# A decode attention kernel: x loaded once, first on the sync queue, its rows rebuilt on chip, and the last values load cut in two

## The chip, the cores and the metric

The kernel runs on one core of a Trainium2 chip. The metric is the device time of one execution in microseconds (us). Lower is better. The engines are named as in the profile: PE (matrix product), DVE (vector), ACT (scalar), POOL (GpSimd) and SP (the engine that only issues transfers here). ACT issues a few transfers as well.

## The reference

One token is decoded through an attention layer and a gating branch that read the same normalised input.

```python
x  = A_x                                   # (1, 1, 512), bf16
xn = layernorm(x)
# attention: 32 heads of 128, the last 4096 positions of the caches
q  = xn @ wq                               # 512 x 4096
s  = attention(q, k_cache[-4096:], v_cache[-4096:]) @ wo
# branch B: with one position the first half (gelu of xn@w1, shifted) is all zeros
x1 = xn + zeros @ w2
b  = x1 + gelu(layernorm(x1) @ w3) @ w4
out = x + s * silu(b)
```

The caches that are read are 32 heads x 4096 positions x 128 numbers, twice, in bf16: 67 MB of the 79 MB that the kernel loads. Everything is read once.

## The kernel before

**Tiling.** The 32 heads are worked in 8 groups of 4 (`G = 4`). For a group the keys come in one load of 4 MB: 128 partitions, each with 128 chunks (`CP = 128`) of 128 numbers, where 32 partitions belong to one head. The values come in the same shape. Part of a group's scores is made on DVE (`k_vector`, L321 multiplies keys by the broadcast query, L323 sums), part on PE (`k_turn`, L339 transposes, ACT copies at L342, `k_scores`, L350 multiplies). Then softmax, and `v_wide` (L427) multiplies values by the probabilities.

**Loop.** `for s in range(NG + LAG)` (L531) works on keys of group `s` and on values of group `s - 2` (`h`). Within the loop the order of PE, DVE and ACT is the written order (a manual schedule); ahead of the loop a scheduler orders the instructions. Each engine runs its own stream in order.

**Queues.** `load` (L75) issues a transfer on SP's queue and keeps the written order: w2, w3, w4, then keys of groups 0 to 2, values 0, keys 3, values 1 and so on. ACT's queue carries three transfers at the very start: `x_bf` (L79, x as 128 partitions x 4), `x_row` (L82, x as 4 rows of 128 on partitions 0, 32, 64, 96, into a tile that POOL has zeroed, L81) and `wq_sb` (L84, 4 MB). Completion is signalled through eight semaphore slots used in turn; a transfer that takes a slot again waits for the one before on it.

**Setup on the engines.** `x_bf` becomes `x_f` (L183), then the first layernorm gives `xn_bf` (L188). PE permutes it (L194, `xq_ps`), zeroes two banks (L145), and multiplies by wq (L208) to make the queries, which are copied, spread and broadcast into `q_bc` (L210 to L216). Branch B multiplies w2 (L233), takes a second layernorm (`z3_bf`, L239), multiplies w3 (L252), applies gelu, multiplies w4 (L270), and ends in `g_row` (L280). `x_row` is used twice: in `xn_row` (L242) and in the last addition (L653). The `wts` pool holds w2, w3, w4 and wq; the first values load reuses its space.

**The end.** The last group's values come in three loads, cut at `cuts = (0, 64, 96, CP)` (L526): 2 MB, 1 MB and 1 MB, followed by two loads of the last rows of wo (`wo_rows`, 256 KB each). The first two pieces go through `v_wide`, the last 32 chunks through `v_part` (L461), which multiplies one chunk per product:

```python
def v_part(g, v, c0, c1):
    s = st[g]
    for c in range(c0, c1):
        nc.tensor.matmul(s["oT"][:], lhsT=v[:, c, :], rhs=s["pT"][:, c, :], start=False,
                         stop=(c == CP - 1), skip_group_check=True)
```

Ahead of it on PE stand the transposes of the first pieces' sum (`v_turn`, L444) and eight products that add the other heads' output (L155 with `y_sum`). Behind it come `v_out` on DVE (L471), four heads' products with `wo_rows` (L155), the multiplication by `g_row` (L651), the addition of `x_row` (L653) and the store.

Of the kernel before, what the change touches and what calls it, by code (L numbers as in the profile page):

```python
# [8 lines left out]
P = 128  # L9
BF16 = mybir.dt.bfloat16  # L10
FP32 = mybir.dt.float32
ACT = mybir.ActivationFunctionType
ALU = mybir.AluOpType
AX = mybir.AxisListType
# [12 lines left out]
def kernel(  # L27
# [14 lines left out]
    nc = tc.nc  # L42
# [9 lines left out]
    CP = G * W // P  # L52
    PB = P // G
    KC = D // P
# [9 lines left out]
    small = ctx.enter_context(tc.tile_pool(name="small", bufs=1))  # L64
    ps_misc = ctx.enter_context(tc.tile_pool(name="ps_misc", bufs=1, space=PSUM))
# [7 lines left out]
    wts = wts_guard.__enter__()  # L73

    def load(dst, src):  # L75
        return tc.keep_in_program_order(nc.sync.dma_start(out=dst, in_=src))  # L76

    x_bf = small.tile([P, KC], BF16, name="x_bf")
    nc.scalar.dma_start(out=x_bf[:], in_=A_x.rearrange("a b (p c) -> p (a b c)", p=P))  # L79
    x_row = small.tile([P, P], BF16, name="x_row")  # L80
    nc.gpsimd.memset(x_row[:], 0.0)  # L81
    nc.scalar.dma_start(out=x_row[0:P:32, :], in_=A_x.rearrange("a b (j n) -> (a b j) n", j=KC))  # L82
    wq_sb = wts.tile([P, KC, HD], BF16, name="wq_sb")
    nc.scalar.dma_start(out=wq_sb[:].rearrange("p c n -> p (c n)"),  # L84
                        in_=A_wq.rearrange("(a b c) n -> b a (c n)", a=4, c=KC))
# [17 lines left out]
    ident_bf = const.tile([P, P], BF16, name="ident_bf")  # L103
# [12 lines left out]

    sel = wts.tile([P, PB, G], BF16, name="sel")
    nc.vector.tensor_copy(out=sel[:], in_=ident_bf[:, 0:P:32].unsqueeze(1).to_broadcast([P, PB, G]))
    ind = const.tile([P, 1], FP32, name="ind")
    nc.vector.tensor_reduce(out=ind[:], in_=ident_f[:, 0:P:32], axis=AX.X, op=ALU.max)  # L120
    neg_half = const.tile([P, 33], FP32, name="neg_half")
# [66 lines left out]
    nc.vector.tensor_copy(out=xn_bf[:], in_=xn_f[:])  # L188


    perm = wts.tile([P, P // 4, 4], BF16, name="perm")
    nc.vector.tensor_copy(out=perm[:], in_=ident_bf[:].rearrange("k (a b) -> k b a", a=4))
    xq_ps = ps_tr.tile([P, KC], FP32, tag="pt", name="xq_ps")
# [9 lines left out]
    for b in range(2):  # L203
        zeros(qr[b][:])
        for c in range(KC):
            wc = wq_sb[:, c, :].rearrange("p (g a d) -> p g a d", a=G, d=Dh)
            for a in range(G):
                nc.tensor.matmul(qr[b][32 * a:32 * a + 1], lhsT=xq_bf[:, c:c + 1], rhs=wc[:, 4 * b:4 * b + 4, a, :],  # L208
                                 start=False, stop=(c == KC - 1), skip_group_check=True)
    nc.scalar.copy(out=q_row[:, 0:4, 0, :], in_=qr[0][:])  # L210
    nc.vector.tensor_copy(out=q_row[:, 4:8, 0, :], in_=qr[1][:])  # L211
    for b in range(2):
        qb_ps = ps_tr.tile([P, 4, Dh], FP32, tag="pt", name="qb_ps")
        nc.tensor.matmul(qb_ps[:], lhsT=sel[:].rearrange("k b a -> k (b a)"), rhs=q_row[:, 4 * b:4 * b + 4, 0, :],
                         start=True, stop=True)
        nc.scalar.copy(out=q_bc[:, 4 * b:4 * b + 4, :], in_=qb_ps[:])  # L216
    for b in range(2):
# [5 lines left out]
        for t in range(2):  # L223
            rows = slice(64 * t, 64 * t + 64)
            nc.scalar.copy(out=q_pair[rows, 4 * b:4 * b + 4, :, G * t:G * t + G].rearrange("p g l a -> p g a l"),
                           in_=qt_ps[rows].bitcast(BF16).rearrange("p g (a m l) -> p g a m l", a=G, l=2)[:, :, :, 0, :])
# [4 lines left out]
    for j in range(KC):  # L231
        for c in range(KC):
            nc.tensor.matmul(hs_ps[:, j:j + 1], lhsT=w2_sb[:, c, j::4],  # L233
                             rhs=shifted_bf[:, c:c + 1], start=(c == 0), stop=(c == KC - 1))
# [30 lines left out]
    for i in range(11):  # L265
        n = P if i < 10 else 96
        terms.append((a_bf[0:n, i % 3, i // 3:i // 3 + 1], w4_sb[0:n, i, :]))
    for i, (col, w) in enumerate(terms):
        r = 32 * (i % 4)
        nc.tensor.matmul(hr_ps[r:r + 1].rearrange("r j n -> r (j n)"), lhsT=col, rhs=w, start=False,  # L270
                         stop=(i >= len(terms) - 4), skip_group_check=True)
# [25 lines left out]
                            op=ALU.max)  # L297
    par_t = const.tile([1 + G, PB, G], FP32, name="par_t")
    nc.vector.tensor_scalar(out=par_t[:],
                            in0=ident_f[0:1 + G, 1:1 + G].unsqueeze(1).to_broadcast([1 + G, PB, G]),  # L300
# [222 lines left out]
        rows_add(y_ps, o_blk[3][:, h - h_part:h - h_part + 1], wo_row(h), h == H - 1)  # L523

    NG = H // G
    cuts = (0, 64, 96, CP)  # L526
    region = tc.manual_schedule(engines={mybir.EngineType.PE, mybir.EngineType.DVE,
                                         mybir.EngineType.Activation})
    region.__enter__()
# [155 lines left out]
```

## Time and profile before

| | us |
|---|---|
| runs, median of 3 | 193.44 (193.44 to 193.47) |
| profiled execution, span from the first to the last instruction | 191.2 |
| what lies outside the span (median less span) | 2.2 |
| DVE busy | 150.9 (79% of the span) |
| PE busy | 116.4 (61%) |
| ACT busy | 89.2 (47%) |
| POOL busy | 2.3 (1%) |
| bytes moved by DMA | 79.02 MB, mean 413 GB/s |
| mean granted clock of PE | 0.72 |

The profile gives a span for the profiled execution and no separate device time for it, so the median stands for that. DMA's load does not appear among the engines' busy times: a line of the page gives the mean busy share of its 16 engines in 40 slices of the span, another what they moved in GB/s. In the timeline and the chain of waits, the first number of a line is its start in us from the span's start and the second what it took.

### The profile page before, as it was taken

Reading aid. Unit: us, or ns where it says so; the run is one execution under the profiler, and the core shown is the slowest. Engines: PE = TensorE matmul, PEld = TensorE weight load, DVE = VectorE, ACT = ScalarE, POOL = GpSimd, SP = SyncE. Lnnn points to the kernel's source line nnn. Section 1 sums busy time; section 2 is a strip of 40 time slices with the busy share of each in tenths; the row PEclk is TensorE's granted clock in tenths of the full one; section 3 lists DMA queues with packets and bytes.
Section 4 is the critical chain, followed back from the end, with each engine's and each line's share of the span. In section 5 each row is a group of like instructions: output and inputs, shape, how many; then the busy total and the mean of one; then the engine's idle time right before and its main releaser. Section 6 shows DMA issues by size and latency. Waiting matters only on the chain.

```text
span 191.2 us, 2839 instructions
## 1 busy us (share of the span) xinstructions
PE 116.4 (61%) x1159; PEld 74.2 (39%) x1159; DVE 150.9 (79%) x175; ACT 89.2 (47%) x191; POOL 2.3 (1%) x11
## 2 busy tenths in 40 slices
PE   1653754989825368256845772680888189739762
PEld 0430222767614334143334441540763077313322
DVE  1660159979999999999999999999999999980111
ACT  2001370888794076427464564542475148733120
POOL 2110000000000000000000000000000000000000
PEclk9999695555755557955695588557567858975998
DMA  6999999999999999999999999999999998999990
GB/s 211 447 430 404 431 418 439 439 439 437 432 434 439 432 429 432 432 439 432 422 432 432 418 422 418 452 439 435 439 432 434 435 432 372 471 425 405 420 371 32
DMA packets 4572, 79.02 MB, mean 413 GB/s; under 512 B 624, under 2 KB 1232, under 8 KB 1488
## 3 DMA queue, kind: packets, MB, share of 16 engines
q1 hardware_dynamic: 4264, 74.65, 91.6%
q10 hardware_dynamic: 296, 4.20, 5.1%
q8 instruction: 9, 0.15, 0.3%
q14 instruction: 3, 0.02, 0.0%
HBM read 78.84 MB, written 0.00 MB: 412 GB/s over the span
## 4 chain that ended last, share of the span: by engine, by line
DVE 46%; DMA 43%; PE 5%; ACT 3%; issue 1%; SPq 1%; ACTq 0%; DVEq 0%
DMA kv<-in_A_k_cache_dram 31%; DVE S L323 28%; DVE prod L321 15%; DMA kv<-in_A_v_cache_dram 10%; ACT kt L342 3%; DMA x_bf<-in_A_x_dram 2%; PE pt L339 2%; PE ov L427 1%; DVE m L366 1%; DVE S L364 1%; SPq L76 1%; PE sT L350 1%; DVE mx L374 1%; PE oT L461 1%; PE ot_ps L444 0%
## 5 line engine op out<-in xcount | busy, mean ns | idle before, releaser
L323 DVE TENSOR_REDUCE S<-prod 128x20 f32<-128x2560 bf16 (+1 forms) x32 | 86.0, 2686 | 1.1
L342 ACT COPY kt<-pt 128x1024 bf16<-128x1024 bf16 x52 | 51.2, 1013 | 40.4 <-PE pt L339 38.7
L339 PE MATMUL pt<-ident_f,kv 128*128 128x128 f32 x208 | 46.7, 376 | 10.8 <-DMA kv<-in_A_k_cache_dram 10.8
L321 DVE TENSOR_TENSOR prod<-kv,q_bc 128x2560 bf16<-128x2560 bf16 (+1 forms) x32 | 45.4, 1418 | 3.9 <-DMA kv<-in_A_k_cache_dram 3.7
L339 PEld LDWEIGHTS pt<-ident_f,kv 128*128 128x128 f32 x208 | 34.2, 196 | 14.4 <-DMA kv<-in_A_k_cache_dram 10.5
L350 PE MATMUL sT<-q_pair,kt 128*128 128x8 bf16 x416 | 19.4, 170 | 15.7 <-ACT kt L342 15.5
L350 PEld LDWEIGHTS <-kt 128*128 128x128 bf16 x416 | 16.4, 104 | 26.8 <-ACT kt L342 25.8
L427 PE MATMUL ov<-kv,pT 128*16 128x512 bf16 x248 | 22.0, 515 | 1.4 <-DMA kv<-in_A_v_cache_dram 1.4
L388 ACT ACTIVATE pT<-S,mb 128x128 bf16<-128x128 f32 x32 | 13.9, 573 | 0.3
L372 PE MATMUL mt_ps<-ident_f,m 128*1 128x128 f32 x8 | 2.9, 359 | 17.4 <-DVE rden L399 16.9
L433 ACT COPY ov_sb<-ov 128x512 f32<-128x512 f32 x8 | 4.7, 586 | 17.1 <-PE ov L427 17.1
L427 PEld LDWEIGHTS <-pT 128*16 128x16 bf16 x248 | 6.9, 109 | 13.2 <-issue 11.4
L359 ACT ACTIVATE own<-sT,par 128x48 f32<-128x48 f32 (+1 forms) x32 | 7.5, 356 | 3.7 <-PE sT L350 3.7
L444 PE MATMUL ot_ps<-ident_f,ov_sb 128*128 128x128 f32 x32 | 7.1, 359 | 2.9 <-ACT mb L384 1.9
L211 DVE CAST q_row<-qr_ps 128x512 bf16<-128x512 f32 x1 | 0.7, 692 | 9.9 <-PE qr_ps L208 9.9
L388 ACT ACTIVATION_READ_ACCUMULATOR pT<-S,mb 128x1 f32 x32 | 8.3, 258 | 0.0
L372 PEld LDWEIGHTS mt_ps<-ident_f,m 128*1 128x1 f32 x8 | 0.6, 80 | 17.9 <-DVE rden L399 17.2
L399 DVE RECIPROCAL rden<-den_ps 128x4 f32<-128x4 f32 x8 | 1.4, 175 | 7.0 <-PE den_ps L394 7.0
L381 PE MATMUL mb_ps<-md,par_t 5*128 5x4 f32 x16 | 3.9, 311 | 4.1 <-DVE md L376 4.1
L255 ACT ACTIVATE a_row<-a_ps 128x384 bf16<-128x384 f32 x1 | 0.5, 491 | 12.0 <-remote 12.0
L444 PEld LDWEIGHTS ot_ps<-ident_f,ov_sb 128*128 128x128 f32 x32 | 4.5, 178 | 3.9 <-ACT mb L384 2.3
L208 PE MATMUL qr_ps<-wq_sb,xq_bf 128*1 128x512 bf16 x32 | 3.1, 566 | 3.7 <-DMA wq_sb<-in_A_wq_dram 3.7
(122 smaller groups left out, 81.6 us busy)
## 6 DMA issues: line engine op xcount, KB each, us to landing
kv<-in_A_k_cache_dram SPq DMA_DIRECT2D x7, 4096.0 KB, 31.3
kv<-in_A_v_cache_dram SPq DMA_DIRECT2D x7, 4096.0 KB, 30.6
wq_sb<-in_A_wq_dram ACTq DMA_DIRECT2D x1, 4096.0 KB, 17.6
kv<-in_A_k_cache_dram SPq DMA_DIRECT2D x2, 2048.0 KB, 27.4
wo<-in_A_wo_dram SPq DMA_DIRECT2D x1, 2048.0 KB
kv<-in_A_v_cache_dram SPq DMA_DIRECT2D x1, 2048.0 KB
kv<-in_A_v_cache_dram SPq DMA_DIRECT2D x2, 1024.0 KB, 17.6
w_sb<-in_B_w_dram SPq DMA_DIRECT2D x1, 1376.0 KB, 9.1
```

What stands on the lines that cost most here:

```text
L321: nc.vector.tensor_tensor(out=prod[:, 0:m, :], in0=kn[:, rows, :], in1=q_bc[:, g:g + 1, :].to_broadcast([P, m, Dh]), op=ALU.mult)
L323: nc.vector.tensor_reduce(out=st[g]["S"][:, rows], in_=prod[:, 0:m, :], axis=AX.X, op=ALU.add)
L339: nc.tensor.transpose(pt[:, i, :], kn[:, c:c + 2, :].rearrange("p c d -> p (c d)").bitcast(FP32), ident_f[:])
L342: nc.scalar.copy(out=kts[b][:, 0:n, :], in_=pt[:, 0:n, :].bitcast(BF16))
L350: nc.tensor.matmul(st[g]["sT"][:, c:c + 2, :].rearrange("p c a -> p (c a)"), lhsT=kt[:, i, l::2], rhs=q_pair[:, g, l, :], start=(l == 0), ...
L359: nc.scalar.mul(s["own"][:, 0:m, a], s["sT"][:, 0:m, a], par[:, a:a + 1])
L372: nc.tensor.transpose(mt_ps[:], s["m1"][:], ident_f[:])
L381: nc.tensor.matmul(mb_ps[:], lhsT=par_t[:].rearrange("k b a -> k (b a)"), rhs=md[:], start=True, stop=True)
L388: nc.scalar.activation(out=s["pT"][:, :, a], in_=s["S"][:], func=ACT.Exp, scale=scale, bias=mb[:, a:a + 1], accum_out=s["sum"][:, a:a + 1])
L427: nc.tensor.matmul(ov[r:r + 4 * G], lhsT=s["pT"][:, c:c + 4, :].rearrange("p i a -> p (i a)"), rhs=v[:, c:c + 4, :], start=(i < 4), stop=( ...
L433: nc.scalar.copy(out=s["ov_sb"][:], in_=ov[:])
L444: nc.tensor.transpose(ot_ps[:, step * j:step * j + P], s["ov_sb"][:, j, :], ident_f[:])
```

## The change

`x_bf` is loaded by the first transfer on SP's queue. The transfer of `x_row` and the zeroing ahead of it are gone: DVE builds two masks from the identity, spreads `x_bf` by one of them, and one product on PE with the other gives x's four rows, each repeated on 32 partitions; DVE copies them into `x_row`. On ACT, wq is the first and only transfer. The last load of values is cut at chunk 112 into two loads of 512 KB, and `v_part` waits for the second only at chunk 112.

```diff
     x_bf = small.tile([P, KC], BF16, name="x_bf")
-    nc.scalar.dma_start(out=x_bf[:], in_=A_x.rearrange("a b (p c) -> p (a b c)", p=P))
-    x_row = small.tile([P, P], BF16, name="x_row")
-    nc.gpsimd.memset(x_row[:], 0.0)
-    nc.scalar.dma_start(out=x_row[0:P:32, :], in_=A_x.rearrange("a b (j n) -> (a b j) n", j=KC))
+    load(x_bf[:], A_x.rearrange("a b (p c) -> p (a b c)", p=P))
...
+    slot = wts.tile([P, PB], BF16, name="slot")
+    nc.vector.tensor_reduce(out=slot[:], in_=ident_bf[:].rearrange("k (a b) -> k b a", a=4), axis=AX.X, op=ALU.max)
+    part = wts.tile([P, 4], BF16, name="part")
+    nc.vector.tensor_reduce(out=part[:], in_=ident_bf[:].rearrange("k (a b) -> k a b", a=4), axis=AX.X, op=ALU.max)
+    same = wts.tile([P, 4, PB], BF16, name="same")
+    nc.vector.tensor_copy(out=same[:], in_=part[:].unsqueeze(2).to_broadcast([P, 4, PB]))
...
+    x_spread = wts.tile([P, PB, KC], BF16, name="x_spread")
+    nc.vector.tensor_tensor(out=x_spread[:], in0=x_bf[:].unsqueeze(1).to_broadcast([P, PB, KC]),
+                            in1=slot[:].unsqueeze(2).to_broadcast([P, PB, KC]), op=ALU.mult)
+    xr_ps = ps_misc.tile([P, P], FP32, tag="misc", name="xr_ps")
+    nc.tensor.matmul(xr_ps[:], lhsT=same[:].rearrange("k a b -> k (a b)"),
+                     rhs=x_spread[:].rearrange("k b c -> k (b c)"), start=True, stop=True)
+    x_row = small.tile([P, P], BF16, name="x_row")
+    nc.vector.tensor_copy(out=x_row[:], in_=xr_ps[:])
...
-    cuts = (0, 64, 96, CP)
+    cuts = (0, 64, 96, 112, CP)
```

The scheduler also moves instructions ahead of the loop. On PE, `rows_open` of `y_ps` (L149), the new product, the permutation (L194) and the two zeroing products (L145) now stand ahead of the 16 products with w2 (L233), where they stood behind them. On DVE the new instructions stand among the masks and around the copies of the first layernorm's result. From L208 on the streams of PE, DVE and ACT are as before, but for the added wait in `v_part`.

## The prediction

> **What bounds the kernel now.** I read the utilisation by slices first, then the same by windows, then the timeline at both ends and the chain of waits. The slices say that the DMA engines are full from the second slice to the last but one, near 430 GB/s:
>
> ```profile
> DMA  6999999999999999999999999999999998999990
> GB/s 211 447 430 404 431 418 439 439 439 437 432 434 439 432 429 432 432 439 432 422 432 432 418 422 418 452 439 435 439 432 434 435 432 372 471 425 405 420 371 32
> ```
>
> DVE is as busy in slices 10 to 34, and the chain of waits runs along DVE from 41.9 to 130 us. That is no contradiction: the two run side by side at nearly one pace, and both must be watched. The end goes by DMA. The chain's last pieces:
>
> ```profile
> 167.79 18.54 DMA kv<-in_A_v_cache_dram
> 186.33 0.05 issue
> 186.38 0.97 PE oT L461 x32
> 187.35 0.02 issue
> 187.37 0.17 DVE o L471
> 187.55 0.04 issue
> 187.59 0.42 PE y_ps L155 x16
> ```
>
> So the time is: when the stream of bytes starts, plus 79 MB at a fixed rate, plus the tail behind the last values (186.33 to 191.2). In the middle nothing is edited. The change can act only on the start, on the tail, and on DVE's start if that slips too far. The start by windows (busy sums per engine, granted clock, DMA share, GB/s):
>
> ```profile
> 0.00:2.00 2.00, 0.61 (x1) 0.10 (x1) 0.52 (x6) 0.00 (x0) 1.23 (x9) 1.00 0.24 29
> 2.00:4.00 2.00, 0.00 (x0) 0.00 (x0) 0.00 (x0) 1.04 (x1) 0.00 (x0) 1.00 0.93 306
> 4.00:6.00 2.00, 0.59 (x2) 0.50 (x2) 0.53 (x4) 0.24 (x1) 0.00 (x0) 1.00 1.01 419
> ```
>
> Between 2 and 4 us the engines are 93% busy but move 306 GB/s. By the packet records, w2's 4 KB packets take 0.159 us each once running, but the first on each engine takes 0.34 to 0.85. This start-up loss is about 0.6 us per engine. The timeline gives the issues and the consumers:
>
> ```profile
> 0.73 1.81 SPq L76 DMA_DIRECT2D w_sb<-in_B_w_dram  x4
> 0.74 0.40 ACTq L79 DMA_DIRECT2D x_bf<-in_A_x_dram  x1
> ...
> 1.18 1.11 ACTq L82 DMA_DIRECT2D x_row<-in_A_x_dram  x1
> ...
> 2.32 0.61 ACTq L84 DMA_DIRECT2D wq_sb<-in_A_wq_dram  x1
> ...
> 4.71 0.17 DVE L183 CAST x_f<-x_bf 128x4 f32<-128x4 bf16 x1 [3.38 <-DMA x_bf<-in_A_x_dram]
> ...
> 19.91 3.15 PE L208 MATMUL qr_ps<-wq_sb,xq_bf 128*1 128x512 bf16 x32 [3.74 <-DMA wq_sb<-in_A_wq_dram]
> ...
> 26.09 1.23 DVE L321 TENSOR_TENSOR prod<-kv,q_bc 128x2048 bf16<-128x2048 bf16 x1 [2.19 <-DMA kv<-in_A_k_cache_dram]
> ...
> 41.91 1.49 DVE L321 TENSOR_TENSOR prod<-kv,q_bc 128x2560 bf16<-128x2560 bf16 x1 [0.99 <-DMA kv<-in_A_k_cache_dram]
> ```
>
> DVE waits 2.19 us for the first keys and 0.99 us for the second load, then no more until 154 us.
>
> **Part 1: x and wq change queues.** ACT loses two DMA issues, so wq is issued near 0.74 instead of 2.32. On SP, x_bf takes the place at 0.73 and pushes w2, w3, w4 and the keys back by one issue, 0.4 us. What counts is when every engine has bulk packets. Before: packet records show w2's first packets at 1.74 to 2.06 (mean 1.87, 0.6 us behind the issue's end), plus 0.62 us of start-up loss: 2.49. The windows give the same: 29, 306 and 419 GB/s over 2 us each are 1.51 MB by 6.00, which at 430 take 3.51 us. After: nothing shows how soon ACT's wq would deliver. The near bound is w2's lag (first packet at 1.75, mean 1.9); the far one is x_bf's row on ACT, whose first packet came at 2.35, 1.2 us behind its issue's end. w2, now second on SP, caps that near 2.3. With wq's 32 KB packets the loss falls on the first packet alone, 0.4 by w2's first ones. So 2.3 to 2.7 against 2.49: between -0.2 and +0.2 us. I take -0.05, the middle.
>
> **Part 2: who shares the engines early.** Before, wq's packets start at 6.6, behind x_row; w2 and most of w3 have passed. Packet records show the two queues taking turns one packet at a time (8 bytes of x_bf, 4096 of w2, 8, 4096; later 32 KB of wq, 10 KB of w4). wq's 32 KB packets take 1.22 us. [...] After: eight wq packets per engine alternate with eight of w2, so w2 lands near 2.5 + 7 or 8 x (1.22 + 0.16) + 0.4 = 12.6 to 14 instead of 4.5; wq lands near 14 instead of 19.9. The first keys stay at 26, since the bytes ahead of them are the same.
>
> This is the dangerous part, as PE runs in order: the w2 products (L233), the second layernorm and the w3 products (L252) stand ahead of L208. From the rows: L233 starts with w2, +0.85 to x1, +4.5 to z3 (8.47 to 12.97; less now, as the zeroing products have moved ahead), +0.3 and 2.9 for L252, then L208 to q_bc 5.1 (19.91 to 25.02). Sum 13.4, so DVE could begin at 26.0 to 27.5 instead of 26.09. Of up to 1.4 us, 0.99 is taken by the wait before 41.91. At most 0.5 us reaches the last group, where PE waits 1.02 us for the last value load's first piece (181.50) after its warm-up products. Cost: nothing. Without that cover it is one for one.
>
> New waits: the second key load now waits for wq's completion, with the third key load and all values behind it on SP; 14 us is early, as SP's queue then holds bytes until past 30. x_f waits for x_bf as before.
>
> **Part 3: x_row on chip.** Two reductions (0.28 to 0.37, rows of L131 and L136), two copies (0.19 and 0.3), one product on DVE (0.35) and one on PE (0.27): some 1.5 us of DVE. It has no work from 14 to 20 us (the windows show 0.00), so this is hidden; without that cover it delays q_bc. The memset of x_row leaves an idle POOL.
>
> **Part 4: the halves.** The last 1 MB becomes two loads of 512 KB; the first lands some 1.2 us before 186.33. But PE is not free then. Its rows:
>
> ```profile
> 185.22 0.66 PE L444 MATMUL ot_ps<-ident_f,ov_sb 128*128 128x128 f32 x4 [0.69 <-ACT ov_sb L433]
> ...
> 185.81 0.40 PE L155 MATMUL y_ps<-y_sum,ind 128*1 128x128 f32 x8
> ...
> 186.38 0.96 PE L461 MATMUL oT<-pT,kv 128*128 128x4 bf16 x32 [0.17 <-DMA kv<-in_A_v_cache_dram]
> ```
>
> PE gets to L461 at 186.21, so of the 0.48 us that sixteen products take only 0.17 can be saved. Then the next is late: the second wo_rows load, issued at 169.1 and 18.5 in landing, arrives at 187.6, and y_ps needs it for its last two heads, from 187.59 + 0.20. Packets halve from 8 KB to 4 KB: 0.309 against 2 x 0.159 us, eight times per engine, so everything behind lands 0.08 later. Heads 30 and 31 then start at 187.73 instead of 187.79. Gain 0.06; bounds 0 and 0.17. [...]
>
> **Sum.** -0.05 - 0.06 = -0.11: a span of 191.1 instead of 191.2. The medians lie 2.2 us above the span (193.44), so 193.3, from -0.2 - 0.17 to +0.2: 193.05 to 193.65.
>
> **Rivals.** *x waits behind wq (slower).* If wq's packets are there as early as x_bf's, the turns put up to seven 1.22 us packets between x_bf's eight per engine: x lands near 2 + 8.5 + 0.5 = 11 instead of 4.7. PE meets L194 and the zeroing before L233, 5.7 us behind x, so from x at 8.3 on it decides. At 11 to 12.5, L233 starts at 17 to 18, DVE at 30 to 31.5; less 0.99 and less PE's 1.02 to 1.5 the end moves by 1.5 to 3: 195.5. For it: both issues start within 0.01 us. Against: x_bf came 0.6 us behind w2 at equal issue, time enough for 8-byte packets of 0.009 us. [...]
>
> *A late stream or a longer chain (slower).* wq comes as late as 2.35, its packets also lose time, w2 does not fill in; or Part 2's chain is 1.5 us longer than summed. Either costs 0.4 to 1: 194.0.
>
> *The start-up loss goes (faster).* wq delivers at 1.75 while x still slips through, with long packets losing 0.25: 2.1 instead of 2.49, -0.4, with the tail 192.9.
>
> *The halves do nothing*, wo_rows gating all: within the forecast.
>
> **Numbers.** Forecast 0.45, late x 0.17, late stream or chain 0.16, no start-up loss 0.22. About 0.2% (0.39 us) is what a measurement here can tell from no change: 193.05 to 193.83. Faster takes the early stream and the forecast's lower edge, 0.25; slower takes late x and most of the late stream, 0.30; same 0.45. The range 192.8 to 195.0 leaves out most of the late-x case and little below.
>
> **What would show it.** Right: x_f starts near 3 us, wq lands near 14, L233 starts at 12.6 to 14, DVE's first prod by 27.5, last values within 0.25 us of 186.33, L461 split by a wait, y_ps ending near 187.95. Wrong: x_f after 8 us; the first prod after 28; L427's wait at 181.5 gone; or 0 to 4 us moving clearly more or fewer than 0.67 MB.

## The result and the profile after

The change makes the kernel a little slower. Its median is 193.88 us (193.39 to 195.21, 22 runs) against 193.48 (193.13 to 193.95, 22 runs of before on the same chip); the ratio is 1.0031, 95% interval 1.0019 to 1.0042. Seven of the 22 runs took 194.3 us or more, and none of before's did. These seven are called the late runs below.

The profiled execution of after took 194.16 us, its span 192.0. The slices of the span, the mean busy share of the 16 DMA engines and what they moved, show a stream as full as before:

```profile
DMA  6999999999999999999999999999999999999980
GB/s 232 396 415 428 441 423 435 430 437 433 437 439 437 437 420 437 423 437 437 427 430 437 423 433 410 457 437 427 437 423 416 433 437 396 466 433 403 411 342 8
```

The start by windows (busy time of PE, its weight loads, DVE, ACT, POOL; granted clock, DMA share, GB/s) and by the timeline:

```profile
0.00:2.00 2.00, 0.61 (x1) 0.10 (x1) 0.52 (x6) 0.62 (x1) 1.09 (x8) 1.00 0.03 0
2.00:4.00 2.00, 0.59 (x2) 0.50 (x2) 0.72 (x5) 0.66 (x1) 0.00 (x0) 1.00 0.87 275
4.00:6.00 2.00, 0.72 (x3) 0.53 (x3) 1.28 (x9) 0.00 (x0) 0.55 (x1) 1.00 1.32 561
```

```profile
0.73 0.62 ACTq L81 DMA_DIRECT2D wq_sb<-in_A_wq_dram  x1
...
0.73 0.39 SPq L76 DMA_DIRECT2D x_bf<-in_A_x_dram  x1
...
2.50 0.17 DVE L186 CAST x_f<-x_bf 128x4 f32<-128x4 bf16 x1 [1.16 <-DMA x_bf<-in_A_x_dram]
...
14.74 0.69 PE L244 MATMUL hs_ps<-shifted_bf,w_sb 128*128 128x1 bf16 x16 [6.95 <-DMA w_sb<-in_B_w_dram]
...
26.23 1.23 DVE L332 TENSOR_TENSOR prod<-kv,q_bc 128x2048 bf16<-128x2048 bf16 x1 [1.12 <-ACT q_bc L227]
...
42.19 1.49 DVE L332 TENSOR_TENSOR prod<-kv,q_bc 128x2560 bf16<-128x2560 bf16 x1 [1.13 <-DMA kv<-in_A_k_cache_dram]
```

x is there 2.2 us earlier than before. w2's 4 KB packets take turns with wq's 32 KB packets, 1.21 us each, and w2 lands at 14.69. The queries are ready 0.1 us behind the first keys (26.13), and DVE still has a wait of 1.13 us ahead of the second load. So the start is nearly what it was. The end is not. The chain of waits no longer ends on the values:

```profile
187.23 0.95 PE oT L472 x32
...
188.20 0.17 DVE o L482
...
188.42 0.42 PE y_ps L158 x16
```

The last values landed at 186.44, 0.11 us later than before, but PE came to them at 187.23. Before, it had waited for them. PE's rows of two earlier steps, the values of group 5 (L427 before, L438 after) and the first piece of the last values, show the lateness on its way, before first and then after:

```profile
164.60 1.90 PE L427 MATMUL ov<-kv,pT 128*16 128x512 bf16 x32
...
181.50 1.04 PE L427 MATMUL ov<-kv,pT 128*16 128x512 bf16 x16 [1.02 <-DMA kv<-in_A_v_cache_dram]
```

```profile
166.49 3.26 PE L438 MATMUL ov<-kv,pT 128*16 128x512 bf16 x32
...
183.04 1.04 PE L438 MATMUL ov<-kv,pT 128*16 128x512 bf16 x16
```

Before, the second row waited 1.02 us for data. In after it waits for none. The granted clock, the share of its full clock that PE was allowed (1.00 full, 0.50 half), was 0.50 from 152.2 to 169.3; before it had risen to 1.00 at 159.0. The windows of before (the third number from the end is the granted clock):

```profile
153.00:160.00 7.00, 6.19 (x50) 5.27 (x50) 6.86 (x9) 3.79 (x4) 0.00 (x0) 0.57 0.97 421
160.00:166.00 6.00, 4.80 (x83) 3.17 (x85) 5.53 (x7) 5.02 (x9) 0.00 (x0) 1.00 1.00 422
```

### The profile page after: what moved, and what is told of

The parts are those of the page before. It is cut to its first block, busy times and chain, and to the rows that moved or that the text cites. A ratio compares the mean times of both kernels' runs of the same rounds, so it can differ in the third digit from the quotient of the medians.

```text
span 192.0 us, 2845 instructions
## 1 busy us (share of the span) xinstructions
PE 118.7 (62%) x1160; PEld 75.4 (39%) x1160; DVE 152.2 (79%) x180; ACT 89.0 (46%) x191; POOL 2.2 (1%) x10
## 4 chain that ended last, share of the span: by engine, by line
DVE 47%; DMA 34%; PE 14%; ACT 3%; issue 1%; ACTq 0%; SPq 0%; DVEq 0%
DVE S L334 28%; DMA kv<-in_A_k_cache_dram 26%; DVE prod L332 15%; DMA wq_sb<-in_A_wq_dram 7%; PE ov L438 3%; PE pt L350 3%; PE yr_ps L529 2%; ACT kt L353 2%; PE ot_ps L455 2%; PE wm L518 1%; PE sT L361 1%; DVE S L375 1%; DVE m L377 1%; DVE mx L385 1%; ACT ov_sb L444 1%
## 5 line engine op out<-in xcount | busy, mean ns | idle before, releaser
L350 PE MATMUL pt<-ident_f,kv 128*128 128x128 f32 x208 | 47.5, 381 | 10.4 <-DMA kv<-in_A_k_cache_dram 10.4
L350 PEld LDWEIGHTS pt<-ident_f,kv 128*128 128x128 f32 x208 | 34.7, 198 | 13.9 <-DMA kv<-in_A_k_cache_dram 10.0
L438 PE MATMUL ov<-kv,pT 128*16 128x512 bf16 x248 | 24.3, 559 | 0.0
L438 PEld LDWEIGHTS <-pT 128*16 128x16 bf16 x248 | 7.2, 116 | 13.6 <-issue 12.7
L392 PEld LDWEIGHTS mb_ps<-md,par_t 5*128 5x128 f32 x16 | 3.3, 259 | 5.7 <-PE sT L361 4.2
```

The lines of the kernel that those rows point to most:

```text
L350: nc.tensor.transpose(pt[:, i, :], kn[:, c:c + 2, :].rearrange("p c d -> p (c d)").bitcast(FP32), ident_f[:])
L392: nc.tensor.matmul(mb_ps[:], lhsT=par_t[:].rearrange("k b a -> k (b a)"), rhs=md[:], start=True, stop=True)
L438: nc.tensor.matmul(ov[r:r + 4 * G], lhsT=s["pT"][:, c:c + 4, :].rearrange("p i a -> p (i a)"), rhs=v[:, c:c + 4, :], start=(i < 4), stop=( ...
```

## The experiments

All were compared with before on one chip in each group. Theory C says that PE's granted clock in the last keys' stage decides; the rivals stand in the expectations.

**Each half of the change alone.** `e1_halves` is before with after's cuts, `e2_x_only` is after with before's cuts.

```diff
-    cuts = (0, 64, 96, CP)
+    cuts = (0, 64, 96, 112, CP)
```

> The kernel before with only the last values load cut in two. Theory C (the granted clock of PE while the last keys are worked decides, and the early part of the change moves it): as before, 193.4, within 0.1 to 0.15 either way; last values at 186.4, L461 not before 186.2, so at most 0.17 won. Rival H (the halves themselves cost, by one more transfer and one more wait): 193.8, the whole loss.

> The changed kernel with the old cuts: only x, its rows and the queues are changed. Theory C: 193.8 to 193.9 with a wide spread, as the whole change; the products with the values of group 5 (L427 of before) start near 166 instead of 164.6 in runs that are late. Rival S (only the stream's later start counts): last values 0.1 later than before and 193.55. Rival H: 193.4.

Measured: the halves 193.79, ratio 1.0020 (1.0009 to 1.0032); x alone 193.80, ratio 1.0026 (1.0008 to 1.0044). For x alone that is what theory C said, and three of its twelve runs are late ones (up to 194.94). For the halves it is not: theory C said 193.4, within 0.15, and the median is the 193.8 of rival H. None of their runs is a late one, but three of twelve stand at 194.19 to 194.26, above all 35 runs of before in this group (up to 193.98). The end of the profile with the halves:

```profile
186.04 0.95 PE L461 MATMUL oT<-pT,kv 128*128 128x4 bf16 x32
187.25 0.72 PE L155 MATMUL y_ps<-wo_rows,o 128*1 128x128 bf16 x16 [0.26 <-DVE o L471]
```

The product of the last chunks starts 0.34 us earlier than before (186.38), and the sixteen products behind it then take 0.72 instead of 0.39, because the second load of `wo_rows` lands at 187.54. They end at 187.97, as before (187.98). So the halves gain nothing in this execution, which took 193.49. Why the median of this kernel is 0.2% up is not in its profile and stays open; f1 below, which has the halves too, shows no such cost.

**The early part in another order.** `e3_row_on_chip` is after with `x_bf` first on ACT, wq second there, and the old cuts. `e6_wq_on_sp` is after with wq on SP between w3 and w4.

```diff
-    load(x_bf[:], A_x.rearrange("a b (p c) -> p (a b c)", p=P))
+    nc.scalar.dma_start(out=x_bf[:], in_=A_x.rearrange("a b (p c) -> p (a b c)", p=P))
```

> x_row is made on chip, but x_bf stays the first load of ACT's queue, wq behind it, old cuts. x_bf takes turns with w2 as before, so w2 lands near 4.5 and L233's products run near 7. Theory C: the early PE work is back at its old place, so 193.4 to 193.5 with before's spread. If the making of the rows on DVE and PE costs: 193.8. If the missing x_row lets wq start near 4 instead of 6.6, nothing of it is seen at the end, since the engines were full.

> The kernel after with wq as a load of the SP queue between w3 and w4 instead of the first load of the ACT queue, so that x, w2, w3, wq, w4 and the keys follow each other in one queue and nothing shares the engines with w2. w2 lands near 5 us instead of 14.7, wq near 15 to 19, the second layernorm is as early as in before. With x_bf at 0.73 and w2 at 1.14 the first 4 KB packets come at 2.3, 0.4 us later than in before, and no other transfer fills that time: stream 0.3 later than in before, last values near 186.6. Theory C with the late w2 as what moves the clock: the runs above 194.3 are gone, median 193.7 to 193.9, by the stream alone. Rival (the late w2 has no part in them, the on-chip rows or the place of x has): the upper runs stay and the median is 194.0 or more.

Measured: e3 193.60, ratio 1.0005 (0.9994 to 1.0016); e6 193.71, ratio 1.0007 (0.9996 to 1.0019). In both w2 is there before 5 us, and neither has a run over 194.3 (their highest are 194.14 and 194.29). Making the rows on chip costs nothing that these runs can tell. PE can be late in this order too: in e3's profile, which took 193.93, the clock stayed at half from 151.2 to 178.5 and PE came to the last chunks at 186.83, 0.85 us behind their data, which had landed early (185.98). e6 pays with a stream that lands 0.3 us later (186.63).

**PE kept busy ahead of the last keys.** `e4_warm_before_keys` is after with eight zero products in front of the last group's keys.

```diff
+            if s == 7:
+                warm(8)
```

> The changed kernel with eight products of zeros on PE where it waits for the last keys (149 to 153.5 us), so that PE isn't idle there. Theory C: PE gets the full clock for the last keys (153.7 to 166), the products with values of group 5 start by 164.7, the end hangs on the last values again: 193.3 to 193.5, and narrow. If the clock isn't what makes it late: 193.9 or more, as the change.

Measured: 193.77, ratio 1.0024 (1.0008 to 1.0040), with a run of 195.22. That lies between theory C's 193.3 to 193.5 and the 193.9 of a loss that the clock doesn't make, so neither is borne out. In its profile, of an execution of 193.48, the clock was full from 149.6 to 163.2 and then half until 176.9, so the keys went quickly and the values of group 5 started at 164.58 but took 3.59 us. So in this execution, with PE fed earlier, the half clock lay at 163.2 to 176.9 instead of the 152.2 to 169.3 of the first profile of after; it wasn't gone.

**The comparison itself, and work taken off PE's way.** `f0_unchanged` is before. The other two are after and before with a quarter of the products for group 5's values; the other 24 of 32 are left out.

```diff
-                v_wide(h, v)
+                v_wide(h, v, 32)
                 sm_exp(s - 1)
```

> The kernel before, unedited, run as one of the compared kernels. Every kernel tried so far, whatever its edit, had its fastest run 0.2 to 0.35 us above the fastest run of before (193.34 to 193.48 against 193.13), although before has about three times as many runs. If the comparison itself is fair, the ratio is 1.000 with an interval that holds it, median 193.45 and fastest run about 193.2. If kernels in the compared place run a little longer for a reason that is not in their code, this one shows it too: 193.6 to 193.7, ratio 1.001 or more, and the ratios of all other experiments must be read against it.

> The kernel after, with only 32 of the 128 chunks of the values of group 5 multiplied (v_wide(5) has 8 products instead of 32; the other chunks' share is left out). Its 24 products stood on the chain from the last keys to the exponentials of groups 6 and 7 and so to v_wide(6): 1.9 us at full clock, 3.3 us at half. Nothing else moves, the loads least of all. Theory C (the late runs of after are runs in which TensorE at half clock comes late to the last values): the slack is now 1.4 to 2.4 us more, so the runs above 194.3 are gone, the products of the first piece of the last values wait for it in the profile, and the median is 193.5 to 193.6, 0.1 to 0.15 above the same cut in before. Rival S (the stream itself is late in those runs, TensorE has no part): median 193.85 and the runs above 194.3 stay. Rival H (the halves cost by themselves at the very end): no run above 194.3 but the median stays 0.2 to 0.3 above the same cut in before.

> The kernel before with the same cut: only 32 of the 128 chunks of the values of group 5 multiplied. Theory C: before already has slack in most runs, so the median falls little, 193.35 to 193.45, and the spread becomes narrower, since the upper runs (193.6 to 194.0) are those in which TensorE comes late. Rival S: no change, median 193.45 and the same spread of 0.8 us, which then is the stream's.

Measured: f0 193.44, ratio 1.0001 (0.9989 to 1.0013), so the comparison is fair. With the cut, after takes 193.53 (193.33 to 194.1), ratio 1.0004 (0.9993 to 1.0014), and before 193.53 (193.28 to 193.76), ratio 1.0000 (0.9991 to 1.0010). The late runs are gone and the two kernels are equal. The loads are untouched by this cut, so the loss of after goes through PE. One thing is missing for a full proof: after itself was not run on this chip, so that its late runs would have appeared there is taken from the other chips. Two parts of the expectations missed. In f1's profile (193.99) the first piece of the last values is not waited for: of the 2.2 us saved on group 5's values 0.6 is left at those of group 6 (178.30 instead of 178.90), and PE comes to the last chunks 0.38 us behind their data. And before with the cut is not faster: 193.35 to 193.45 was expected. The profile of f0 shows that before itself isn't always in time:

```profile
166.06 3.13 PE L427 MATMUL ov<-kv,pT 128*16 128x512 bf16 x32
...
182.42 1.04 PE L427 MATMUL ov<-kv,pT 128*16 128x512 bf16 x16
...
186.60 0.94 PE L461 MATMUL oT<-pT,kv 128*128 128x4 bf16 x32
```

Same kernel as in the first profile, clock 0.50 until 168.6, no wait at the first piece, and the last product 0.34 us behind its data (186.26). It took 193.54.

**The queries earlier, and the whole work in a better order.** `g1_after_short_w3` is after with a quarter of w3's products. `g2_early_wide` is e3, and `i3_after_early_wide` is after, with `y_wide(0)` moved into PE's idle time.

```diff
-    for c in range(KC):
+    for c in range(1):
         wc = w3_sb[:, c, 0:10 * P].rearrange("p (q r) -> p r q", r=10)
```

```diff
...
                 y_open()
+                y_wide(0, False, 0, 8)
...
             ox_pick(1)
+            y_wide(0, False, 8, 12)
             sm_turn(NG - 1)
+            y_wide(0, False, 12, 16)
...
-            y_wide(0, False)
-            warm(3)
+            warm(4)
```

> The kernel after with 5 of the 20 products of w3 (only the first of four chunks; the rest of the MLP's inner sum is left out). They stand on TensorE ahead of the products of wq, so q_bc is ready 1.5 to 2 us earlier, about 24.5 instead of 26.24, before the first keys land at 26.1; the loads and the last stage are unedited. Rival Q (in the late runs of after, 194.4 to 195.2, the chain from the late w2 to q_bc is so late that DVE starts on the keys over 1 us late and stays late): the runs above 194.3 are gone, median 193.5 to 193.6. Theory C (in those runs TensorE is late in the last stages by its clock alone): the late runs stay, about one in three, median 193.8 to 193.9.

> The kernel of the run with the row on chip (x_bf and wq on ACT, the last values in the old three pieces, earliest stream of all: last values at 185.98), with the sixteen products of y_wide(0) moved from the place right ahead of the warm-up products and v_wide(6) into TensorE's idle time before (eight after y_open, four after ox_pick(1), four after sm_turn of the last group) and four warm-up products instead of three. This takes 1.9 us at half clock, less one more warm-up product of 0.4, off the way to v_wide(6). Theory C: TensorE is then in time for the last values in nearly all runs, the end hangs on the stream, and the stream is 0.3 earlier than in before: median 193.1 to 193.3. Rival (the clock falls with the work moved, or the stream in most runs isn't earlier): 193.5 or more.

> The kernel after, whole, with the sixteen products of y_wide(0) moved into TensorE's idle time between v_turn(5) and the last group's maxima, and four warm-up products instead of three ahead of v_wide(6): 1.9 us less, 0.4 more, on TensorE's way to v_wide(6). If TensorE's lateness in the last stages is what after loses, the late runs are gone or rare and the median is 193.5 to 193.6, no worse than before by more than the later stream (0.13). If the stream itself is what is late in them, they stay at one in three.

Measured: g1 194.19, ratio 1.0038 (1.0017 to 1.0058); four of twelve runs are over 194.3, up to 195.47, so a late chain to the queries isn't the cause. Its profiled execution, 195.47, was a mixed one: the stream was 0.7 us late (187.14), and PE came 1.29 us behind that. g2 193.49, ratio 1.0006 (0.9993 to 1.0019): no gain over before, and its stream landed at 186.28, not at e3's 185.98; that early stream was a draw, not a property. One of its twelve runs took 194.64, so w2 before 5 us doesn't rule such a run out. i3 193.77, ratio 1.0015 (1.0003 to 1.0028), one run of eleven over 194.3: fewer than in after, which eleven runs don't prove, and not cured. In its profile PE still comes 0.38 us behind the data. No version beat before.

**Four more executions of after.**

> The kernel after once more, for another profiled execution. About one run in three of it takes 194.4 to 195.2; the profiled execution so far took 194.16. If this one is such a run, its profile tells the two theories apart. Theory C: DVE starts on the keys within 0.3 us of 26.2 and on the last keys within 0.5 of 154.2, the last values land by 186.6, and TensorE at half clock begins v_wide(6) 1 us or more later than 178.9. Rival Q: DVE's first product of keys begins at 27.3 or later and its wait before 42.2 is gone. Rival S: the last values land after 187.

> The same as the look before it, for a third profiled execution of after: with one run in three late, one of the two looks is late in five cases of nine. A run of 193.4 to 193.9 instead shows the other end: TensorE waiting for the last values, at full clock for part of the last keys' stage.

> The kernel after, another profiled execution, in the hope of a late one (194.3 to 195.2, one in three). In a late one: if TensorE's clock alone makes it, the last values land by 186.6 and the products of the last part start 1 us or more behind them; if the stream makes it, the last values land at 187 or later and the sixteen landings of the first keys already spread over 0.8 us or more instead of 0.45. Both together would look like the run with w3's products cut: 187.14, and 1.28 behind that.

> The same, a further execution of after, with the same two readings for a late run.

Measured, with the earlier executions; the gap is the start of the last chunks' products less the landing of the last values (in after these are the last 16 chunks only, and the products begin on the 16 ahead of them, so the gap can be negative):

| execution | time | clock full again at | values of group 5 start | last values land | gap |
|---|---|---|---|---|---|
| h2 | 193.56 | 157.7 | 164.90 | 186.49 | -0.17 |
| h1 | 193.58 | 159.1 | 165.06 | 186.50 | -0.16 |
| after, first | 194.16 | 169.3 | 166.49 | 186.44 | 0.78 |
| j2 | 194.51 | 169.9 | 166.28 | 186.22 | 1.34 |
| j1 | 194.79 | 170.2 | 166.56 | 186.52 | 1.32 |
| f0 (before) | 193.54 | 168.6 | 166.06 | 186.26 | 0.34 |

PE's rows in h1, and then in j2:

```profile
165.06 1.90 PE L438 MATMUL ov<-kv,pT 128*16 128x512 bf16 x32
...
181.63 1.04 PE L438 MATMUL ov<-kv,pT 128*16 128x512 bf16 x16 [0.92 <-DMA kv<-in_A_v_cache_dram]
```

```profile
166.28 3.59 PE L438 MATMUL ov<-kv,pT 128*16 128x512 bf16 x32
...
183.38 1.04 PE L438 MATMUL ov<-kv,pT 128*16 128x512 bf16 x16
...
187.56 0.94 PE L472 MATMUL oT<-pT,kv 128*128 128x4 bf16 x32
```

The one run of before beside j1 and j2 took 194.18, more than any of the 22 above, so j1 and j2 are best compared with h1 and h2, the same kernel. This settles what these late runs are. In j2 the data were 0.3 us earlier than in h1, and the run is 0.9 us longer. Stream and queries have no part in it: DVE began at 26.11 in j2 and at 26.30 in h1. What counts is the stage of the last keys: in h2 the clock fell back to half from 164.5 to 167.9 and the values of group 5 took 3.36 us, but they had started 1.6 us earlier than in the first profile of after, and the run wasn't late.

**What turns the clock.** e1's profile and j2's have the clock's steps at the same places to 0.1 us from 74 to 152.9, and their last keys start at 153.51 and 153.49. Their rows agree to 0.02 us up to ACT's fifth copy of keys in this stage (first e1's two pairs, with the granted clock of 160 to 166 us by windows, then j2's):

```profile
157.95 2.16 ACT L342 COPY kt<-pt 128x1024 bf16<-128x1024 bf16 x2 [1.36 <-PE pt L339]
160.87 2.16 ACT L342 COPY kt<-pt 128x1024 bf16<-128x1024 bf16 x2 [0.76 <-PE pt L339]
```

```profile
160.00:166.00 6.00, 4.95 (x65) 3.94 (x67) 4.75 (x6) 4.25 (x6) 0.00 (x0) 0.74 1.01 427
```

```profile
157.93 2.16 ACT L353 COPY kt<-pt 128x1024 bf16<-128x1024 bf16 x2 [1.36 <-PE pt L350]
161.14 1.93 ACT L353 COPY kt<-pt 128x1024 bf16<-128x1024 bf16 x2 [1.05 <-PE pt L350]
```

```profile
160.00:166.00 6.00, 4.91 (x50) 3.91 (x49) 4.48 (x6) 4.04 (x5) 0.00 (x0) 0.50 1.00 420
```

j2's copy comes 0.27 us later, PE waits 0.30 us for it, and where e1's clock rises at 163.2, j2's stays at half until 169.9. The time from the third copy to the fifth sorts the profiles: at half clock 2.91 or 2.92 us in f0, f2, e1, e3 and g2, 3.19 to 3.21 in after, j1, j2, f1, g1 and i3; at full or rising clock 2.23 in before and e6, 2.5 to 2.6 in h1, h2, e2 and e4. Up to here the late copy goes with x on SP and wq alone on ACT. But it doesn't go with the clock: f0, f2 and e3, without it, stayed at half until 168.6 or later, and h1, h2 and e2, with it, rose by 159.7.

The traces hold something that sorts the clock better. All its steps in an execution lie on one grid of 3.41 us, and where this grid lies against the last keys differs between executions of one kernel. The table orders all profiles but e4 (which feeds PE just there) by the time from the last line of the grid to PE's first transpose of the last keys:

| grid line to last keys, us | profiles | clock full again at |
|---|---|---|
| 0.58 to 0.66 | e1, g2 (copy on time) | 163.2 |
| 0.60 to 0.65 | j1, j2, g1 (copy late) | 169.9 to 170.8 |
| 0.93 to 1.46 | before, h1, e2, i2, k1 | 159.0 to 161.2 |
| 1.50 to 2.20 | after, f0, f1, f2, e3, i3 | 168.6 to 179.6 |
| 2.81 to 2.92 | h2, e6, i1 | 157.7 to 158.1 |

In the last three rows late copies and punctual ones stand together, in two of them before and after as well. In the first profile of after the clock failed to rise at its line at 159.0, 2.3 us ahead of the late copy (161.35); in before it rose at the same line. So the place of the grid goes with the clock nearly everywhere, and the late copy can have turned it only at 0.58 to 0.66. This is an order found afterwards, in 19 profiles; no run set the grid. Where the clock stayed at half, PE came to the last chunks at 186.60 in f0 and 186.83 in e3, and at 187.23 to 187.84 in after, j1 and j2: a stage at half clock costs after more.

Three runs asked why the copy is late. `i1` loads wq in four 1 MB pieces on ACT. `i2` is before with the last 48 partitions of w2 loaded behind w3. `k1` is after with one early copy of one column on ACT, two instructions with its table load.

```diff
+    fill = small.tile([P, 2], FP32, name="fill")
+    nc.scalar.copy(out=fill[:, 0:1], in_=ind[:])
```

> The kernel after with wq as four loads of 1 MB on the ACT queue, 8 KB packets instead of 32 KB. x_bf and w2 stand where after has them and wq still shares the engines with w2 from the start, but w2 waits for 8 KB packets only: w2 lands near 2.5 + 8 x (0.31 + 0.16) + 0.4 = 6.7 instead of 14.7, and no engine can be left behind by a 32 KB packet. Theory W (the late w2 is what makes the late runs, through TensorE's early work and the clock): they are gone, median 193.55. Theory E (the shared start leaves one engine behind): the early lag is 8 KB's worth, 0.3 us instead of 1.2, so they are fewer as well, and the landings of the first keys spread over 0.25 us instead of 0.45. If the late runs stay, both are wrong and the place of x or the rows made on chip must be the cause.

> The kernel before with the last 48 of the 128 rows of partitions of w2 loaded behind w3 instead of ahead of it; three packets per engine that take turns with wq's 32 KB packets, so that w2 is complete near 13 to 15 us instead of 4.5, as in after, while the start of the stream (w2's first part, then w3, wq behind x_row) is that of before. Theory W: late runs appear as in after, one in three over 194.3, median 193.7 to 193.9. Theory E: none appear, 193.45 to 193.55.

> The kernel after with one copy of one column on ScalarE, early, while ScalarE is idle (with the table load that it brings, two instructions more). Every later instruction of ScalarE then has the same number in ScalarE's stream as in before, while the loads and w2's lateness stay as in after. Theory A (the pause of 0.28 us ahead of the fifth copy kt<-pt of the last keys belongs to a place in ScalarE's stream of instructions, and it decides whether the clock rises): third to fifth copy 2.92 us at half clock (2.2 to 2.3 at full) instead of 3.20 (2.5 to 2.6), the runs above 194.3 are gone, median 193.5 to 193.6, what the later stream alone costs. Rival W (the pause and the late runs come with the late w2): 3.20, one run in three above 194.3, median 193.8 or more.

Measured: i1 196.60, ratio 1.0149 (1.0119 to 1.0178); i2 195.27, ratio 1.0088 (1.0062 to 1.0113); k1 194.81, ratio 1.0075 (1.0057 to 1.0093). None of the three times answers the question. In i1 the scheduler put most of wq's products ahead of w2's; DVE began the second load's keys at 45.12 instead of 42.19, with no wait left, and the last chunks' products started 2.9 us later than in before (189.27). In i2 the stream itself fell to 343 GB/s between 13 and 19 us (before: 388), and the last values landed at 188.41. In k1 the last values landed at 187.59, 1.15 us later than in after; the first keys were already 0.97 us late (27.10), for a reason that its profile doesn't show. But the profiles answer in part. A late w2 goes with 2.23 us from the third copy to the fifth in k1 (w2 at 15.44) and in i2 (its rest at 16.52), so the pause doesn't come with w2; in k1 it went away with the two instructions. That speaks for a place in ACT's stream of instructions; single profiles, and at a rising clock. That the pause makes late runs rests on the five profiles of the table's first two rows, and was not tried by itself. Why after has more late runs than before is so far open.

## Why the prediction was wrong

**Part 1, the stream's start, held within its bounds**, on the other side of zero. Forecast -0.05, bounds -0.2 to 0.2. In five executions of after the last values landed at 186.22 to 186.52, mean 186.43; before, f0 and f2 give 186.33, 186.26 and 186.35. That is 0.12 later. The first 4 us moved 0.55 MB instead of 0.67, one of the signs of being wrong: wq's first packets came at 2.13 to 2.79, nearer to the bound of the x_bf row than to w2's.

**Part 2 held up to its last sentence.** w2 at 14.69 (said: 12.6 to 14, so 0.7 beyond), wq at 14.51 (near 14), DVE at 26.23 (26.0 to 27.5), 1.13 us of wait left at 42.19. Then: "At most 0.5 us reaches the last group, where PE waits 1.02 us for the last value load's first piece (181.50) after its warm-up products. Cost: nothing." This step failed. Little did reach the last group (DVE began its keys at 154.21 instead of 154.07), but the 1.02 us was no property of the kernel. It was the cover in one execution, in which the clock had risen at 159.0. In f0, the same kernel, the wait is gone and the gap is 0.34 us. A cover that hangs on the granted clock was spent as if it were fixed. The list of signs named it ("L427's wait at 181.5 gone"), without a price: with the cover gone PE came 0.78 us behind the data in the first profile of after and 1.3 us in j1 and j2.

**Part 3 held**: e3 makes the rows on chip at a ratio of 1.0005 (0.9994 to 1.0016).

**Part 4 held in the profile of e1**: `wo_rows` gates, gain 0 within the bounds of 0 to 0.17. By the runs it didn't: the halves alone are 0.2% up (0.17 to 0.62 us by the interval), where nothing or a gain was summed. The cause stays open.

**The rivals.** x came at 2.50, so the late x fell. The late stream was right in sign and worth 0.12, not 0.4 to 1, and the faster start didn't come. A rival in which PE ends last was missing. It would have had its place (the last keys at half clock), its price (3.59 less 1.90, what the same 32 products took at 89.96 and at 164.60, plus the slower transposes ahead, four in 1.09 us at half clock against 0.64 at full) and its point (the wait of 1.02 us) in the trace of before: 160 to 166 us at clock 1.00 behind 153 to 160 at 0.57.

## The clock in the runs

What I had not expected is how sharply this clock cuts. It was 0.50 or 1.00, in steps a multiple of 3.41 us apart (in the first profile of before 3.41, 6.83, 10.24, 13.65 and 20.48 us), and where the steps lay could differ between executions of one kernel: one is at 152.2 in the first profile of before, at 151.5 in f0. In one pair (e1 and j2) a shift of 0.3 us on another engine goes with the next 7 us of it, and so with 1 us of the kernel; in the other groups of the table the place of the steps goes with it alone.

The 1.3 us by which PE comes behind the data in j1 and j2 are 0.7% of 192 us. That is ten times the change's own effect on the stream (0.12), and it decided the sign here.

In j2 PE was busy 6.26 of the 7 us from 153 to 160, mostly with transposes, at clock 0.50, and the clock stayed at half until 169.9. In the first profile of before PE was busy 6.19 of the same 7 us with the same work, and the clock rose at 159.0. So PE's busy time there doesn't tell the two apart. What does was not tried in any run.

A second surprise: a load of keys or values has 16 landings, and what needed it started behind the last of them: DVE at 26.09 on the first keys, whose last landing is at 25.99, and PE at 186.38 on the last values, whose last is at 186.33 (first profile of before). These landings lie further apart at the end: the sixteen of the first keys lie 0.45 us apart (25.54 to 25.99), those of the last values 2.02 us (184.31 to 186.33). An early imbalance can last or not: g1 has 0.90 us at the first keys and 2.51 at the last values, with an end 0.7 us later than in after, but e6 has 1.77 and then 1.98.

## What to carry to other kernels

When a transfer bounds a kernel and TensorE waits for it by a microsecond, read the granted clock under that wait before spending it: here, at half clock for most or all of them, the 32 products of group 5's values took 3.13 (f0) to 3.59 us (j2) instead of 1.90, and nothing was left of a wait of 1.02. Take the cover from several executions, since one profile shows one position of the clock's steps. And where a change moves the median by a few tenths of a percent, look at the whole spread first: here the means lie 0.61 us apart (194.10 and 193.49), and half of that is seven runs of 22 that are 0.96 later than the other fifteen (194.75 and 193.79). The other half is spread over those fifteen, which lie 0.30 above before; 0.12 of that is the later stream, and the rest has no row of its own here.
